# Routing of tokens to experts: small operands moved from SBUF to a PSUM bank

## The chip, the core and the metric

The kernel runs on one core of a Trainium2 chip. The core has five engines that work side by side, each on its own list of instructions in order: TensorE (PE, matrix products), VectorE (DVE), ScalarE (ACT), GpSimd (POOL) and SyncE (SP, which issues transfers). SBUF is the working memory of 128 partitions. PSUM is a smaller memory of 8 banks, 2 KB a partition each, into which TensorE writes and which VectorE and ScalarE read and write. The metric is device time in microseconds of one execution, the median of several.

## The reference

Attention with pooled queries, then a mixture of 8 experts with a fixed room of 576 tokens each:

```python
q_pool = q.reshape(B, H, S // 2, 2, D).mean(axis=3)        # B = H = 8, S = 1152, D = 64
scores = q_pool @ k.transpose(0, 1, 3, 2) / sqrt(D)
x = softmax(scores) @ v                                     # -> N = 4608 tokens of 512
logits = x @ w_gate                                         # [4608, 8]
for idx in argsort(-logits.flatten()):                      # best fit first
    tok, e = idx // E, idx % E
    if assigned[tok] >= 0 or counts[e] >= cap: continue     # cap = 576
    assigned[tok] = e; counts[e] += 1
for e in range(E):
    out[assigned == e] = relu(x[assigned == e] @ w1[e]) @ w2[e]
```

All is computed to nearly full fp32 accuracy: a product of two fp32 matrices is made as three products of their upper and lower parts.

## The kernel before

Two stages follow each other: attention (until about 1045 us) and the experts. The change lies in the second, in `experts`.

**Routing without a sort.** The greedy assignment is computed expert by expert, in the order in which experts fill up; `route(k)` finds the k-th expert to fill and its 576 tokens. Token scores lie as 128 partitions x 36 blocks (J = 36) x 8 experts in L. A penalty PEN per expert closes those that are full. `best` (L741 to L745) takes of each token the best open expert: LM = L + PEN, mx = its maximum, T1 = where LM equals mx, times e8 (a number for each expert), and r8 = the largest, which names the expert. `keys` (L747 to L755) turns the 36 scores of a partition into whole numbers with the same order (ki), in two halves of 16 bits, as floats in kf. Then eight search rounds, four on each half, narrow a threshold by one hexadecimal digit each. One round is a chain between VectorE and TensorE:

- VectorE: GE = keys against 16 thresholds (L789, 128x576 numbers); beside the next step it subtracts the threshold found so far from the keys (L820), and once, L824, joins the halves.
- TensorE: counts per expert and threshold, 5 small products into rb (L796).
- VectorE: keeps the own blocks (dg, L800) and adds them up (red, L802). TensorE: sums over partitions (L806).
- VectorE: which experts are full at which threshold (L810), a transpose (fars, L813), the digit found (got, L816, with half32, a table of 5 numbers), whose sum `base` starts the next round's L789.

After eight rounds `close` (L848 to L855) names the expert (re) and its tokens (gt, mine, asg), `members` and `prefix` (G, PS) number them, ST (L912, four operations of 128x640) and 20 small products into tb (L917) look up which token comes at which place, and L921 to L928 write the list idx. `shut`, `taken`, `left` and `settle` (PEN, CAPS, U, room L977) prepare the next expert.

**Products.** For each expert, GpSimd gathers weights and 576 tokens by idx (indirect DMA). ScalarE rounds them to upper parts (W1H, W2H, XH), GpSimd makes the lower parts of the weights by subtraction (W1L, W2L, L1095: 16 subtractions of 128x512 for each expert) and of half of the tokens from the third expert on (XL, L1045); VectorE makes the others. The tokens of the first two experts are turned by TensorE in five blocks (L1002) and subtracted by VectorE (L1011). TensorE then makes the products of the first layer (ph, L1112) and of the second (po, L1142 and L1139).

**Order.** `Order.emit` fixes the order in which each engine gets its instructions: a planner that gives each group a duration in ns and hands groups out as engines that wait for nothing else would begin them. So the routing of expert k+1 is interleaved with the products of expert k. The engines do not reorder: a count on TensorE that waits for GE holds all products behind it.

**PSUM before.** rb (counts and sums) and tb (the lookups, and the fifth token block when tokens are turned by TensorE) are a bank each; ph has four, po two. The eight banks are in use. All operands of the routing chain other than rb and tb lie in SBUF.

Of the kernel before, what the change touches and what calls it, by code (L numbers as in the profile page):

```python
# [26 lines left out]
M = S // 2              # pooled queries of a head  # L27
NKB = S // 128          # key blocks of a head
E, DM, F = 8, H * D, 1024
N = B * M               # tokens  # L30
CAP = N // E
NPAIR = B * H // 2      # pairs of heads: the same head of two batches
NSTEP = 2 * NKB         # key blocks of a pair
NB = 2 * M // 128       # token blocks of a pair of batches
NBLK = N // 128
SHIFT = 16.0 * 8.0 * math.log(2.0)   # weights are carried times 2^8


class Order:
    """Instructions in groups, with the memory that each reads and writes. `emit` hands them out in the  # L40
    order in which engines that wait for nothing else would begin them."""
# [92 lines left out]
# when parts of a pair's work come, in steps; which part goes first (steps) and how long a part's users give it (ns)  # L134
# [16 lines left out]
def routing_tables(nc, pool, ident, jp, scratch, do):  # L151
    """constants of the routing; `scratch`: whole numbers that are needed only here"""
# [31 lines left out]
    def order():  # L184
        V.tensor_scalar(C["before"], jp, 0.0, None, op0=OP.is_gt)                       # [k, m]: k < m
        V.tensor_scalar(C["upto"], jp, 0.0, None, op0=OP.is_ge)                         # [k, m]: k <= m
        V.tensor_copy(C["e8"], it8)                                                     # E - e
        V.tensor_copy(C["pcol"], it["p"])
        V.tensor_copy(C["pcol2"], it["p2"])
    do("DVE", 700, order)  # L190

    def digits():
        for t in range(4):                                          # (1 .. 16) * 16^t; the last never counts
            V.tensor_scalar(C["nib"][:, t], it["16"], float(16 ** t), None, op0=OP.mult)
            V.memset(C["nib"][:, t, 15:16], 3e9)
        V.tensor_scalar(C["nib"][:, 4], it["16"], -1.0, None, op0=OP.add)               # 0 .. 15
        k1 = scratch.bitcast(F32)[:, at:at + 64]
        V.tensor_scalar(k1, it["d"], 0.0, None, op0=OP.is_ge)                           # [16 j + t, 8 j + e]
        V.tensor_scalar(C["diag"], it["d"], 16.0, None, op0=OP.is_lt)
        V.tensor_tensor(C["diag"], C["diag"], k1, op=OP.mult)  # L200
        V.tensor_scalar(it["m"], it["m"], 15, None, op0=OP.bitwise_and)
        V.tensor_scalar(C["same16"], it["m"], 0.0, None, op0=OP.is_equal)               # [16 j + t, 16 r + t]
    do("DVE", 1500, digits)

    def places():
        V.tensor_copy(C["slots"], it["s"])
        V.tensor_copy(C["slot1"], it["s1"])                                             # 1 + slot
        V.tensor_scalar(C["jval"], it["s"][:, :J], 128.0, None, op0=OP.mult)            # 128 j
        for z in range(2):
            V.tensor_copy(C["TAB"][:, z, J + 1:J + 2], it["p"])                         # ranks, offset, partition  # L210
# [4 lines left out]
def attention(ctx, tc, top, kt, qt, v, wg, x_dram, L, npair=NPAIR):  # L215
# [7 lines left out]
    # ---- constants  # L223
# [48 lines left out]
    ndiag = const.tile([128, NB, 64], F32, name="ndiag")            # -1 at [64 + i, i, :]  # L272
# [23 lines left out]
    # ---- exact split of queries and keys into parts of 12 bits  # L296
# [45 lines left out]
    # ---- values in two parts, scaled by a power of two so that half precision's range holds them  # L342
    def values(n, t):
# [4 lines left out]
        # only the power of two counts  # L348
# [18 lines left out]
    # ---- maxima of the scores, [query, key] order  # L367
    NA = AT["na"]       # token blocks whose scores ScalarE moves out; VectorE reads the others in place

    def max_chunk(n, j, c, z, t):  # L370
        i = n % 2
        banks = [(ma, "ma"), (mb, "mb")]
        if n == 0:      # nothing else needs memory yet
# [28 lines left out]
    def aug(n, t):  # L402
# [3 lines left out]
        if n == 0:      # a row of each block of queries  # L406
# [6 lines left out]
        else:           # one row, brought there by DMA  # L413
# [8 lines left out]
    # ---- one key block: scores, weights, weighted values  # L422
    LAG = AT["lag"]

    def step(g):
# [27 lines left out]
        def weighted(js):  # L453
            for j in js:
                # bank 0: blocks 0..2; bank 1: the remainder, block 3
# [6 lines left out]
                for y, z in enumerate((1, 0) if j in (2, 4) else (0, 1)):  # L462
                    # second part times first parts only
# [35 lines left out]
    # ---- the gate's part of two heads, and their columns of x  # L499
# [12 lines left out]
    def gate(n, t):  # L512
        """three groups of columns of TensorE side by side; the sum stays turned until a batch is done"""
# [29 lines left out]
    def gate_last(n, q, t):  # L543
        """the last two heads: added at once"""
# [25 lines left out]
    # ---- the order of things  # L570
    od.cur = None
    for _ in range(AT["wu"]):        # TensorE's clock is up when the first products come
        od.add(-70, "PE", 60, lambda: nc.tensor.matmul(mb[:, :128], ones, ones, start=True, stop=True), w=["mb"])
    for _ in range(AT["wv"]):        # and is still up when the scores come
# [36 lines left out]
    for n in range(1, npair, 2):  # L611
        od.cur = None
        g = NSTEP * n + NSTEP
        if n + 1 < npair:
            # between the heads, when the weighted values' memory is free
# [24 lines left out]
# which work of an expert goes first (f.), how long users give it (ns), how it is divided  # L640
# [5 lines left out]
def experts(ctx, tc, x_dram, L, w1, w2, out, C):  # L646
# [13 lines left out]
    # ---- state of the assignment  # L660
    U = one([128, J], F32, "U")                     # not assigned yet
    asg = one([128, J], BF, "asg")                  # assigned to, as E minus its number
    mine = one([128, J], BF, "mine")
    CAPS = one([128, E], F32, "CAPS")               # room that is left
    PEN = one([128, E], F32, "PEN")                 # closed experts
# [3 lines left out]
    nc.vector.memset(PEN, 0.0)  # L669

# [4 lines left out]
    mx = one([128, J], F32, "mx")  # L675
    r8 = one([128, J], BF, "r8")
# [3 lines left out]
    kf = one([128, 2, J], F32, "kf")  # L680
# [6 lines left out]
    half32 = one([128, 5], F32, "half32")  # L687
# [3 lines left out]
    gt = one([128, 2, J], BF, "gt")  # L691
# [3 lines left out]
    G = one([128, 2, J], F32, "G")  # L695
# [18 lines left out]
    # first parts of 576 tokens, second parts of the last 64 and of the other 512  # L714
# [5 lines left out]
    rb = psum.tile([128, 512], F32, name="rb")  # L720
    tb = psum.tile([128, 512], F32, name="tb")
# [3 lines left out]
    TB = [("tb", c) for c in range(5)]  # L725

    def bj(ap, n=E):        # [128, J] over n
        return ap[:, :, None].to_broadcast([128, J, n])

    def be(ap):             # [128, E] over J  # L730
        return ap[:, None, :].to_broadcast([128, J, E])

    def first_of(mask8, out8, r1):
        """the first expert of a mask, one-hot; r1: E minus its number"""
        V.tensor_tensor(sm[:, 5], mask8, e8[:, 0], op=OP.mult)
# [3 lines left out]
    def best(dve, f):  # L739
        """of each token the best expert that is open, as E minus its number, and how well it fits"""  # L740
# [3 lines left out]
        dve(220, lambda: V.tensor_tensor(T1, T1, e8, op=OP.mult), ["T1"], ["T1"], f)  # L744
        dve(370, lambda: V.tensor_reduce(r8, T1, axis=AX.X, op=OP.max), ["T1"], ["best"], f)  # L745

    def keys(dve, f):  # L747
        """the order of floats as that of whole numbers, in two halves of 16 bits"""
# [3 lines left out]
        dve(106, lambda: V.tensor_tensor(ki[:, 0], ki[:, 0], b, op=OP.bitwise_xor), ["mx", "ki"], ["ki"], f)  # L752
        dve(90, lambda: V.tensor_scalar(ki[:, 1], ki[:, 0], 16, None, op0=OP.arith_shift_right), ["ki"], ["ki1"], f)
        dve(90, lambda: V.tensor_scalar(ki[:, 0], ki[:, 0], 0xFFFF, None, op0=OP.bitwise_and), ["ki1"], ["ki"], f)
# [464 lines left out]
```

## Time and profile before

| | |
|---|---|
| three runs | 1628.81, 1636.2, 1640.48 us, median 1636.2 |
| profiled execution, span | 1634.9 us |
| TensorE busy over the span | 1476.2 us (90%) |
| VectorE busy | 1254.1 us (77%) |
| GpSimd busy | 926.7 us (57%) |
| mean granted TensorE clock | 0.963 |
| expert stage, 1045 to 1635 us: TensorE busy | 506.15 of 590 us |

The trace covers one execution, from the first to the last instruction. A row of a group names line, engine, operation, output and inputs with shapes, the number of instructions, their busy time in us and the mean of one in ns, then the idle time of the engine ahead of them and what ended it. A timeline row gives start and duration in us; in brackets stands how long the engine had been idle and what released it. L numbers are lines of the kernel before.

### The profile page before, as it was taken

The page shows a single profiled execution, that of the slowest core. Times are in us where ns is not written, and L with a number is a line of the kernel's source. Part 1 is how long each engine was busy: PE and PEld are TensorE (multiplying, and loading weights), DVE is VectorE, ACT ScalarE, POOL GpSimd, SP SyncE. Part 2 cuts the span into 40 slices and gives each one's busy share as a digit, 9 for nine tenths or more (in the row PEclk, how much of TensorE's full clock was granted, in tenths as well). Part 3 has the DMA queues.
Part 4 walks back from the last instruction along what each step waited for, and adds up shares of the span by engine and source line. Part 5 has one row for each costly group of instructions (what it writes and reads, how often), then busy time and mean ns, then how long its engine had stood idle before and what let it go on. Part 6 is the DMA issues. An engine that isn't in the chain of part 4 may idle for free.

```text
span 1634.9 us, 32933 instructions
## 1 busy us (share of the span) xinstructions
PE 1476.2 (90%) x12535; PEld 1223.8 (75%) x12535; DVE 1254.1 (77%) x2636; ACT 898.5 (55%) x1801; POOL 926.7 (57%) x821
## 2 busy tenths in 40 slices
PE   7899999999999999999999999779588879899997
PEld 5677877877777777777778778567476767779995
DVE  7998898888888889978989986588887788753310
ACT  4776777777777777767677776222322222233431
POOL 4575566566566657656656666134644554557641
PEclk8999999999999999999999999899898989899999
DMA  9784676667676766856767752032132434333400
GB/s 235 188 184 117 159 175 156 148 155 172 158 162 157 177 141 155 197 126 165 189 135 164 169 112 48 15 132 90 73 139 86 134 127 134 114 116 119 147 30 30
DMA packets 123515, 221.97 MB, mean 136 GB/s; under 512 B 49500, under 2 KB 74076, under 8 KB 121180
## 3 DMA queue, kind: packets, MB, share of 16 engines
q1 hardware_dynamic: 114876, 167.40, 43.6%
q0 software_dynamic: 8336, 52.44, 9.0%
q8 instruction: 99, 1.62, 0.4%
q14 instruction: 60, 0.49, 0.1%
q10 hardware_dynamic: 144, 0.02, 0.0%
HBM read 99.63 MB, written 18.87 MB: 72 GB/s over the span
## 4 chain that ended last, share of the span: by engine, by line
PE 50%; DVE 37%; DMA 6%; issue 4%; ACT 1%; POOL 1%; SPq 0%; another core or an unknown queue 0%; POOLq 0%; DVEq 0%; ACTq 0%
PE av L464 12%; PE ph L1112 11%; PE po L1142 9%; DVE MS L392 6%; DVE PM L448 5%; PE sc L436 4%; DVE MX L380 4%; PE sc L439 4%; PE ma L376 3%; DVE KL L323 3%; PE mb L376 3%; DVE got L816 2%; DVE RS L486 2%; DMA VD<-in_v_dram 2%; DVE QL L303 2%
## 5 line engine op out<-in xcount | busy, mean ns | idle before, releaser
L448 POOL TENSOR_TENSOR PM<-P 128x576 f16<-128x576 f32 x383 | 523.5, 1377 | 295.8 <-ACT P L444 292.1
L464 PE MATMUL av<-V,P 128*128 128x129 f16 (+1 forms) x2880 | 442.8, 225 | 0.7 <-DVE V L363 0.5
L444 ACT ACTIVATE P<-sc 128x576 f32<-128x576 f32 x576 | 370.5, 657 | 93.4 <-PE sc L439 84.0
L464 PE MATMUL av<-V,PM 128*128 128x65 f16 (+1 forms) x2880 | 364.7, 198 | 0.0
L464 PEld LDWEIGHTS <-P 128*128 128x128 bf16 (+1 forms) x2880 | 258.2, 100 | 75.6 <-issue 12.8
L464 PEld LDWEIGHTS <-PM 128*128 128x128 f16 (+1 forms) x2880 | 259.9, 100 | 48.1 <-issue 0.5
L436 PE MATMUL sc<-QA,KA 128*128 128x288 f32 x1152 | 265.0, 312 | 0.1
L439 PE MATMUL sc<-QB,KB 65*128 65x288 f32 (+1 forms) x1152 | 251.0, 300 | 3.9 <-issue 3.9
L392 DVE TENSOR_TENSOR MS<-MS 128x1728 bf16<-128x1728 bf16 (+3 forms) x256 | 232.2, 907 | 12.5 <-ACT MS L384 8.8
L448 DVE TENSOR_TENSOR PM<-P 128x576 f16<-128x576 f32 x193 | 196.7, 1019 | 40.5 <-ACT P L444 40.5
L384 ACT CAST MS<-mb 128x384 bf16<-128x384 f32 x314 | 151.3, 482 | 96.7 <-PE mb L376 94.8
L436 PEld LDWEIGHTS sc<-QA,KA 128*128 128x128 f32 x1152 | 196.6, 193 | 4.8 <-ACT P L444 0.4
L376 PE MATMUL mb<-KH,BD 128*128 128x384 f32 x407 | 158.6, 390 | 38.7 <-DVE MX L380 26.2
L439 PEld LDWEIGHTS sc<-QB,KB 65*128 65x128 f32 (+1 forms) x1152 | 189.6, 193 | 4.1 <-issue 4.1
L376 PE MATMUL ma<-KH,BD 128*128 128x384 f32 x438 | 172.5, 394 | 20.6 <-DVE MX L380 20.3
L1142 PE MATMUL po<-W2H,HX 128*128 128x512 f32 x512 | 166.7, 402 | 0.5 <-ACT OT L1147 0.5
L384 ACT CAST MS<-ma 128x384 bf16<-128x384 f32 x250 | 120.2, 481 | 78.8 <-PE ma L376 75.2
L1112 PE MATMUL ph<-XL,W1H 128*128 128x320 f32 (+1 forms) x512 | 159.8, 312 | 2.1 <-DVE XL L1011 2.1
L1112 PE MATMUL ph<-XH,W1H 128*128 128x320 f32 (+1 forms) x512 | 160.6, 314 | 0.6 <-DVE XL L1011 0.6
L1112 PE MATMUL ph<-XH,W1L 128*128 128x320 f32 (+1 forms) x512 | 160.4, 313 | 0.0
L1117 ACT ACTIVATE HX<-ph 128x256 fp32r<-128x256 f32 (+1 forms) x128 | 52.4, 410 | 192.5 <-PE ph L1112 176.6
L1142 PE MATMUL po<-W2L,HX 128*128 128x512 f32 (+1 forms) x320 | 130.3, 407 | 0.0
(233 smaller groups left out, 2561.7 us busy)
## 6 DMA issues: line engine op xcount, KB each, us to landing
QD<-in_qt_dram SPq DMA_DIRECT2D x32, 576.0 KB
KD<-in_kt_dram SPq DMA_DIRECT2D x64, 288.0 KB
VD<-in_v_dram SPq DMA_DIRECT2D x32, 576.0 KB
KA<-KH SPq DMA_DIRECT2D x64, 288.0 KB
KB<-KH SPq DMA_DIRECT2D x64, 288.0 KB
QA<-QH SPq DMA_DIRECT2D x128, 144.0 KB
KA<-KL SPq DMA_DIRECT2D x64, 288.0 KB
QB<-QL SPq DMA_DIRECT2D x64, 144.0 KB
```

The lines of the kernel that those rows point to most:

```text
L376: od.add(t, "PE", 162, lambda: nc.tensor.matmul(m[:, :384], BD[i][:, j, :], KH[i][:, 384 * c:384 * c + 384], start=True, stop=True), r=[(" ...
L380: od.add(t, "DVE", 465, lambda: nc.vector.tensor_reduce(MX[i][:, j, c:c + 1], m[:, :384], axis=AX.X, op=OP.max), r=[mk], w=[("MX", i, j, c ...
L384: od.add(t, "ACT", 371, lambda: nc.scalar.copy(MS[b][:, j % 3, 384 * c:384 * c + 384], m[:, :384]), r=[mk], w=[("MS", b, j % 3, c)], tag="mc")
L392: od.add(t + .01 * z, "DVE", 72 + .52 * w * rows, lambda w=w: nc.vector.tensor_tensor(m[:, :, :w], m[:, :, :w], m[:, :, w:2 * w], op=OP.ma ...
L436: nc.tensor.matmul(c[:, t, :288], KA[i][:, s, ks], QA[i][:, s, 288 * t:288 * t + 288], start=True, stop=False)
L439: nc.tensor.matmul(c[:, t, :288], KB[i][:kr, s, ks], QB[i][:kr, s, 288 * t:288 * t + 288], start=False, stop=True)
L444: od.add(g + 0.1, "ACT", 531, lambda: nc.scalar.activation(p.rearrange("p (a b) -> p a b", a=2), c[:, :, :288], AF.Exp, scale=1.0 / 16), r ...
L448: od.add(g + 0.2, en, dur, lambda: eng.tensor_tensor(pm, p, hi, op=OP.subtract), r=[("P32", g % NP)], w=[("PM", g % NM)], tag="pm" + "DP"[ ...
L464: nc.tensor.matmul(o[:, D * z:], (hi, pm)[z][:, q0:q0 + w], rhs[:, D * z:], start=first and kb == 0 and y == 0, stop=kb == NKB - 1 and y = ...
L1112: nc.tensor.matmul(p, a[:, d, fs], b[:, d, qs], start=z == 0, stop=z == 11)
L1117: nc.scalar.activation(HH[:, f, qs], p, AF.Relu)
L1142: nc.tensor.matmul(o[:n], a[:, z, q0:q0 + n], b[:, z], start=z == 0 and y == 0, stop=z == 7, skip_group_check=True)
```

## The change

A PSUM bank, `kb`, is set aside for VectorE alone, and pieces of it hold the routing chain's small operands: mine, PEN, mx, r8, kf, half32, gt and G move there from SBUF, and four new pieces are added: e8p and pcolp (copies of a row of e8 and of pcol), sm1 (a second copy of the mask of the expert just closed) and kx (the keys as whole numbers, ahead of their split in two). Each two-input operation of the chain then has at most one input in SBUF. T1 is multiplied by e8p, an fp32 row repeated over the blocks, in place of the bf16 table e8. Of the keys only the upper half is copied to kf; `lower` reads the lower half from ki. ST, room and the token subtractions keep their SBUF operands.

To free the bank, rb and tb become parts of one bank, rt: columns 0 to 127 and 128 to 511. The fifth token block is turned in a bank of the products instead (ph[0][1] for the first expert, ph[0][0] for the second). The planned durations of some of these groups are changed. The rest of the difference is comments that are left out.

```diff
+    kb = psum.tile([128, 512], F32, name="kb")
+    used = [0]
+    def bank(*shape):
+        n = math.prod(shape)
+        x = kb[:, used[0]:used[0] + n]
+        used[0] += n
+        return x.rearrange("p (a b) -> p a b", b=shape[1]) if len(shape) > 1 else x
-    mine = one([128, J], BF, "mine")
+    mine = bank(J)
-    PEN = one([128, E], F32, "PEN")
+    PEN = bank(E)
+    e8p = bank(E)
+    sm1 = bank(E)
+    nc.vector.tensor_copy(e8p, e8[:, 0])
-    mx = one([128, J], F32, "mx")
-    r8 = one([128, J], BF, "r8")
+    mx = bank(J)
+    r8 = bank(J)
-    kf = one([128, 2, J], F32, "kf")
+    kx = bank(J).bitcast(I32)
+    kf = bank(2, J)
-    half32 = one([128, 5], F32, "half32")
+    half32 = bank(5)
-    gt = one([128, 2, J], BF, "gt")
+    gt = bank(2, J)
-    G = one([128, 2, J], F32, "G")
+    G = bank(2, J)
-    rb = psum.tile([128, 512], F32, name="rb")
-    tb = psum.tile([128, 512], F32, name="tb")
+    rt = psum.tile([128, 512], F32, name="rt")
+    rb, tb = rt[:, :128], rt[:, 128:]
+    pcolp = bank(1)
+    V.tensor_copy(pcolp, pcol)
...
-        dve(220, lambda: V.tensor_tensor(T1, T1, e8, op=OP.mult), ["T1"], ["T1"], f)
+        dve(370, lambda: V.tensor_tensor(T1, T1, be(e8p), op=OP.mult), ["T1"], ["T1"], f)
...
-        dve(106, lambda: V.tensor_tensor(ki[:, 0], ki[:, 0], b, op=OP.bitwise_xor), ["mx", "ki"], ["ki"], f)
-        dve(90, lambda: V.tensor_scalar(ki[:, 1], ki[:, 0], 16, None, op0=OP.arith_shift_right), ["ki"], ["ki1"], f)
-        dve(90, lambda: V.tensor_scalar(ki[:, 0], ki[:, 0], 0xFFFF, None, op0=OP.bitwise_and), ["ki1"], ["ki"], f)
-        dve(110, lambda: (V.tensor_copy(kf, ki), V.memset(base, -32768.0)), ["ki", "ki1"], ["key", "base"], f)
+        dve(150, lambda: V.tensor_tensor(kx, ki[:, 0], b, op=OP.bitwise_xor), ["mx", "ki"], ["kx"], f)
+        dve(150, lambda: V.tensor_scalar(ki[:, 1], kx, 16, None, op0=OP.arith_shift_right), ["kx"], ["ki1"], f)
+        dve(150, lambda: V.tensor_scalar(ki[:, 0], kx, 0xFFFF, None, op0=OP.bitwise_and), ["kx"], ["ki"], f)
+        dve(200, lambda: (V.tensor_copy(kf[:, 1], ki[:, 1]), V.memset(base, -32768.0)), ["ki", "ki1"], ["key", "base"], f)
...
-                V.tensor_tensor(W, e8, bj(ru), op=OP.is_equal)
+                V.tensor_tensor(W, be(e8p), bj(ru), op=OP.is_equal)
...
-                        V.scalar_tensor_tensor(kf[:, 0], kf[:, 1], 65536.0, kf[:, 0], op0=OP.mult, op1=OP.add)
+                        V.scalar_tensor_tensor(kf[:, 0], kf[:, 1], 65536.0, ki[:, 0], op0=OP.mult, op1=OP.add)
...
-            V.tensor_tensor(widx[k], re[:, 1:2], pcol, op=OP.add)
+            V.tensor_tensor(widx[k], re[:, 1:2], pcolp, op=OP.add)
...
+                V.tensor_scalar(sm1, e8[:, 0], re[:, 0:1], None, op0=OP.is_equal)
-            dve(340, shut, ["re"] + ([("ST", LT["cs"], 3)] if not k else []), ["PEN", "sm"], LT["fb"])
+            dve(500, shut, ["re"] + ([("ST", LT["cs"], 3)] if not k else []), ["PEN", "sm"], LT["fb"])
-                V.scalar_tensor_tensor(CAPS, sm[:, 1], 1e9, CAPS, op0=OP.mult, op1=OP.add)
+                V.scalar_tensor_tensor(CAPS, sm1, 1e9, CAPS, op0=OP.mult, op1=OP.add)
...
-                     (ph[1][1], [("ph", 1, 1)]), (tb, TB)][c] if not k else (
-                         (ph[c // 2][c % 2], [("ph", c // 2, c % 2)]) if c < 4 else (tb, TB))
+                     (ph[1][1], [("ph", 1, 1)]), (ph[0][1], [("ph", 0, 1)])][c] if not k else (
+                         ph[c // 2 % 2][c % 2], [("ph", c // 2 % 2, c % 2)])
```

Two places of the order show what moves. The first is VectorE at the end of the fourth expert's routing, where the lookup tables ST are made. The kernel before (po and ph numbers name the bank):

```order
L902 COPY of<-rb 128x4
L903 CAST TAB<-rb 128x2
L741 TENSOR_TENSOR LM<-L,PEN 128x288
L912 TENSOR_SCALAR ST<-slots,of 128x640 x4
L970 TENSOR_TENSOR CAPS<-CAPS,rb 128x8
L971 SCALAR_TENSOR_TENSOR CAPS<-sm,CAPS 128x8
L975 SCALAR_TENSOR_TENSOR U<-gt,U 128x36
L977 TENSOR_SCALAR room<-PS,of 128x36
```

The kernel after, whose lines are some 17 higher and where kb stands for every operand in the new bank:

```order
L919 COPY of<-rt 128x4
L920 CAST TAB<-rt 128x2
L758 TENSOR_TENSOR LM<-L,kb 128x288
L929 TENSOR_SCALAR ST<-slots,of 128x640 x4
L1169 TENSOR_TENSOR OT_13596<-po_13602,O_13593 64x512
L1139 SCALAR_TENSOR_TENSOR HX<-ph_13598,HX 128x256
L988 TENSOR_TENSOR CAPS<-CAPS,rt 128x8
L989 SCALAR_TENSOR_TENSOR CAPS<-kb,CAPS 128x8
L938 TENSOR_TENSOR ixf<-slot_164,rt 128x5
```

ST stays where it was, ahead of the same small operations; two operations of the products (OT, HX) now come between, and room comes behind the index operations (L938 to L945). The second place is TensorE at the second expert's fifth token block. Before, it was turned in tb amid the first products:

```order
L796 MATMUL rb<-W,GE 64x32
L1002 MATMUL tb<-ident,XG 128x64 x4
L1112 MATMUL ph_13605<-XH,W1L 128x256
L1112 MATMUL ph_13605<-XH,W1H 128x256
L1112 MATMUL ph_13605<-XL,W1H 128x256
L1112 MATMUL ph_13605<-XH,W1L 128x256
L1112 MATMUL ph_13607<-XH,W1H 128x256
```

After, it is turned in ph_13598, the bank in which the first block was turned:

```order
L1130 MATMUL ph_13600<-XH,W1H 128x256
L1130 MATMUL ph_13600<-XL,W1H 128x256
L1130 MATMUL ph_13600<-XH,W1L 128x256
L1020 MATMUL ph_13598<-ident,XG 128x64 x4
L813 LDWEIGHTS GE
L813 MATMUL rt<-W,GE 128x64
```

The first twelve products go to another bank, ph_13600, ahead of it, and the count follows it instead of standing ahead. Around the search rounds the order keeps its pattern: a count, seven or eight products, the sum over partitions, some sixteen products, the next count (half as many in the second layer).

More of the change, by code (lines that the diff above doesn't have):

```diff
@@ L733, in first_of @@
     def first_of(mask8, out8, r1):
-        V.tensor_tensor(sm[:, 5], mask8, e8[:, 0], op=OP.mult)
+        V.tensor_tensor(sm[:, 5], mask8, e8p, op=OP.mult)
         V.tensor_reduce(r1, sm[:, 5], axis=AX.X, op=OP.max)
```

## The prediction

> **What bounds the kernel now.** I read the page's parts 1 and 2 first, then the expert stage in windows, then who TensorE waits for there, and last the durations of the instructions it waits for. The attention stage ends near 1045 us and the change does not touch it. The windows below (engine busy, then granted clock, DMA share, GB/s) split what follows: 1096 to 1460 us is the stretch in which six experts' routing runs beside the products of the experts before them, 1115.6 to 1126.5 a piece of it without any GpSimd work, and 1470 to 1623 the products of the last three experts, when all routing is done.
>
> ```profile
> core 0: us, PE busy (x) PEld busy (x) DVE busy (x) ACT busy (x) POOL busy (x), PEclk, DMA share, GB/s
> 1096.00:1460.00 364.00, 306.87 (x1940) 257.22 (x1939) 292.45 (x943) 99.14 (x209) 181.54 (x182) 0.92 0.32 108
> 1115.60:1126.50 10.90, 10.90 (x89) 10.23 (x88) 8.66 (x36) 2.46 (x6) 0.00 (x0) 1.00 0.01 2
> 1470.00:1623.00 153.00, 153.00 (x911) 138.27 (x910) 33.94 (x84) 51.82 (x111) 81.55 (x87) 1.00 0.26 88
> ```
>
> Without routing TensorE never pauses and its clock is 1.00. With routing it stands idle 364.00 - 306.87 = 57.1 us, and its mean clock is 0.92. But in the 10.90 us of routing without GpSimd it does not pause either: routing as such costs no idle time. What TensorE waits for between 1096 and 1460 us (total, times, longest):
>
> ```profile
> PE rb L796 <- DVE GE L789: 33.8, 15, 10.2
> PE rb L806 <- DVE red L802: 8.3, 6, 4.2
> PE tb L917 <- DVE ST L912: 4.7, 3, 3.5
> PE rb L796 <- DVE W L782: 4.1, 1, 4.1
> PE rb L878 <- DVE tot L873: 3.2, 1, 3.2
> PE rb L878 <- DVE re L891: 1.9, 1, 1.9
> PE po L1142 <- ACT OT L1147: 0.5, 1, 0.5
> ```
>
> Nearly all of it is VectorE's routing chain. TensorE takes its work in order, so a count (L796) whose masks GE are late holds up the expert products queued behind it. Why the chain is late stands in the durations of its instructions (ns, min/median/max):
>
> ```profile
> L816 DVE SCALAR_TENSOR_TENSOR got<-fars,half x49: 191/193/11398, 1052.0 to 1429.8; 128x32 f32<-128x32 f32 x49
> L820 DVE TENSOR_SCALAR kf<-kf,base x56: 229/243/4986, 1050.0 to 1431.4; 128x36 f32<-128x36 f32 x56
> L789 DVE SCALAR_TENSOR_TENSOR GE<-kf,base,nib x56: 771/819/1767, 1049.2 to 1430.0; 128x576 bf16<-128x576 f32 x56
> L912 DVE TENSOR_SCALAR ST<-slots,of x48: 244/375/5697, 1074.9 to 1451.1; 128x640 f16<-128x640 f16 x28, 128x128 f16<-128x128 f16 x20
> ```
>
> An instruction on 32 numbers takes 0.19 us or 11.4 us. The timeline at the longest shows what else runs:
>
> ```profile
> 1170.17 11.40 DVE L816 SCALAR_TENSOR_TENSOR got<-fars,half 128x32 f32<-128x32 f32 x1
> 1170.46 1.30 POOL L1095 TENSOR_TENSOR W1L<-W,W1H 128x512 fp32r<-128x512 f32 x1
> 1171.72 9.80 POOL L1095 TENSOR_TENSOR W2L<-W,W2H 128x512 fp32r<-128x512 f32 x8
> 1182.49 0.56 PE L796 MATMUL rb<-W,GE 128*128 128x64 bf16 x5 [10.15 <-DVE GE L789]
> ```
>
> It ends (1181.57) as the ninth GpSimd subtraction in a row ends (1181.52): VectorE waits out GpSimd's whole run, and TensorE then waits 10.15 us. The Trainium skill, page "SBUF — State Buffer", section "Who interferes with whom", gives a rule for this: a VectorE instruction with two SBUF inputs, or in a two-port mode, shuts out a GpSimd instruction that reads SBUF and is shut out by it, and one with at most one SBUF input does not contend. By that rule, the trace agrees as to who is hit, but the wait was nine instructions long, 11.4 us, not one of 1.3.
>
> **The change, term by term.** The sum is made on the profiled span, 1634.9 us, 1.3 under the runs' median of 1636.2; savings are taken off the median.
>
> Ceiling: 57.1 us idle, and the clock. A mean of 0.92 over 364 us is 29.1 us of lost rate; spread as the busy time is (306.87/364), it cost work 24.5 us. Together 81.6.
>
> Not touched: the waits for ST (4.7), for re (1.9) and for ScalarE (0.5), 0.6 that the list does not name, and 3.0 of the GE row, where VectorE waits for a ScalarE that has no instruction:
>
> ```profile
> 1277.09 0.71 ACT L1117 ACTIVATE HX<-ph 128x256 fp32r<-128x256 f32 x2 [3.93 <-remote]
> 1277.50 0.42 DVE L1121 SCALAR_TENSOR_TENSOR HX<-ph,HX 128x256 fp32r<-128x256 f32 x1 [2.86 <-ACT HX L1117]
> ```
>
> That is 10.7 us, with a clock share of 24.5/57.1 = 0.43 per us 15.3. Left: 66.3. These are waits behind L816 (half32 goes to PSUM), L820, L824, L851 (kf), L789 (kf), L753, L754 (kx) and L743, L781, L782 (mx, r8, e8p), and in the changed kernel none of them reads two SBUF operands or copies SBUF to SBUF.
>
> Ahead of the window, the second routing starts beside the first token blocks' subtractions:
>
> ```profile
> 1087.96 2.75 DVE L743 TENSOR_TENSOR T<-LM,mx 128x288 bf16<-128x288 f32 x1
> 1090.64 0.68 DVE L1011 TENSOR_TENSOR XL<-ph,XH 128x512 fp32r<-128x512 f32 x1
> ...
> L741 DVE TENSOR_TENSOR LM<-L,PEN 128x288 f32<-128x288 f32 x7 | 3.2, 458 | 0.0
> ```
>
> The first products need XL, queued behind T. T's undisturbed time is that of LM, of the same form (458 ns), so XL comes 2.3 us sooner; I take 2.0.
>
> What VectorE pays for PSUM:
>
> ```profile
> L744 DVE TENSOR_TENSOR T<-T,e 128x288 bf16<-128x288 bf16 x7 | 2.1, 304 | 0.0
> L1011 DVE TENSOR_TENSOR XL<-ph,XH 128x512 fp32r<-128x512 f32 x6 | 4.1, 681 | 0.0
> L1095 DVE TENSOR_TENSOR W1L<-W,W1H 128x512 fp32r<-128x512 f32 x2 | 1.4, 688 | 1.6 <-ACT W1H L1092 1.6
> ...
> L891 DVE TENSOR_SCALAR re<-re x8: 145/148/153, 1074.5 to 1449.1; 128x1 f32<-128x1 f32 x8
> ```
>
> - Reads: a subtraction with one operand in PSUM takes 681 ns, with both in SBUF 688. I take no difference.
> - The product with e loses its 16-bit form: 304 goes to about LM's 458 ns, +0.15 us an expert; in the first expert, where nothing runs beside routing, it is on the path. The Trainium skill, page "VectorE: DVE Perf Modes", section "Why PSUM operands drop a tier", says the same: an operand in PSUM limits fp32 to one element a cycle; by it this costs what the row says.
> - Writes to PSUM by VectorE: no row shows one. From below, an SBUF write's time; from above, a small operation's fixed time paid twice, +0.15 us (re, one number, L891). Some 15 stand in the first expert's path: 0 to 2.2 us; nearest are the 36-number rows, so 0.5. In later experts rounds hide them: kf's subtraction (L820) lies beside the count on TensorE.
> - The second mask, sm1 (+0.1), and one fifth token block turned in a bank of the products (ph instead of tb): there the order puts twelve products between the bank's first use and its second, so about 0.6 of waiting. First expert and this together: 1.4 us. Fewer keys are copied (36 instead of 72), worth nothing here: the copy lies ahead of W's wait.
>
> What still waits, afresh: ST keeps slots in SBUF, room (L977) is an SBUF-to-SBUF scalar operation, and XL of later experts (L1045) subtracts two SBUF operands.
>
> ```profile
> L912 DVE TENSOR_SCALAR ST<-slots,of 128x640 f16<-128x640 f16 x28 | 16.8, 661 | 0.0
> L977 DVE TENSOR_SCALAR room<-PS,of x7: 235/239/1273, 1085.3 to 1443.5; 128x36 f32<-128x36 f32 x7
> L1045 DVE TENSOR_TENSOR XL<-XG,XH 128x512 fp32r<-128x512 f32 x12 | 10.6, 901 | 6.2 <-ACT XH L1041 6.1
> ```
>
> ST waits 28 x (661 - 375) = 8.0 us over seven experts, 1.1 a group, of which 4.7 (0.59) reaches TensorE. Today a blocked key operation ahead often leaves room and XL a free port; now they meet GpSimd themselves. Six groups of room at 1.1: 6.9, less the 1.0 of its largest wait, x 0.59 = 3.5 us, with clock 5.0. The same GpSimd work in a sixth less time raises ST's own share by 1.0. XL: 12 x 0.21 = 2.5 us of waiting may double, 1.5 reaching TensorE.
>
> Rounds without a block still end with TensorE and VectorE close together: one had a gap of 0.21, the row at 1115.6 none.
>
> ```profile
> 1106.32 0.42 PE L796 MATMUL rb<-W,GE 128*128 128x64 bf16 x5 [0.21 <-DVE GE L789]
> ```
>
> Half of that for each of the 21 rounds whose wait goes (15 and 6 in the list): 2.2.
>
> Sum: 66.3 + 2.0 - 1.4 - 5.0 - 1.0 - 1.5 - 2.2 = 57.2. 1636.2 - 57.2 = 1579.0 us. Then TensorE bounds the stage, as it does from 1470 on, and GpSimd can feed it: there it keeps up at 153/3 = 51 us an expert and is busy 81.55 of the 153 us.
>
> **Rivals.**
> - The wait moves to what is left in SBUF. For it: one ST took 5697 ns, and each of the keys' long waits shows what a group that comes in the midst of a run pays. If each of the 13 groups of ST and room waits 4 us, that is 52 us of VectorE, x 0.59 = 31 of TensorE, x 1.43 = 44 with the clock; 4.7 x 1.43 + 5.0 + 1.0 = 12.7 of it are counted above, so 31 more: 1610 us. Against it: the seven groups of ST average 1.1 today.
> - All of it goes, ST's waits falling into TensorE's slack: 1636.2 - 81.6 = 1555, up to 1562.
> - The shared bank. rb and tb now lie in one bank, rt. The Trainium skill, page "PSUM — Partial Sum Buffer", section "PSUM bank collisions raise a hardware error", says that two engines must be kept apart by bank and not by address; by it every count must wait for the index operations' reads of tb and these for the counts. As a mechanism here: up to 1.5 us of reading (L921 to L928) each way, twice for seven experts, 21 us: about 1601. Against it: no such wait stands in today's list, and in the order the next count comes some 20 products or more behind the lookups.
> - Not the operands. If VectorE waited for GpSimd's use of something else, nothing changes: 1636. Against it: VectorE's instructions of one tensor input in the same rounds, beside the same GpSimd runs, never wait:
>
> ```profile
> L813 DVE STREAM_TRANSPOSE fars<-far x49: 163/211/214, 1051.7 to 1429.6; 128x32 f32<-128x32 f32 x49
> L802 DVE TENSOR_REDUCE red<-dg x56: 257/264/274, 1050.9 to 1432.1; 128x8 f16<-128x64 f16 x56
> ```
>
> - Slower: PSUM access by VectorE is dear. Some 2 operations in each of 56 rounds and 15 in each of 7 experts are serial, 217; from 57.2/217 = 0.26 us each the gain is gone, at 0.35 it is 76 us: 1655. Against it: 681 beside 688 ns.
>
> **How the numbers follow.** Forecast 0.66 (its own range 1564 to 1596, by the PSUM writes and by what ST, room and XL do), wait moved 0.12, all gone 0.08, bank 0.05, nothing 0.05, dear PSUM 0.04. From 1560 to 1612 leaves out the last two and most of "all gone", some 0.15. About 1% is what a measurement of this kernel can tell from no change (under 1619.8 is faster): faster 0.66 + 0.12 + 0.08 + 0.05 = 0.91, same 0.05, slower 0.04.
>
> **What the changed profile would show.** Right: the operation that replaces L816 has a maximum under 0.4 us, also beside GpSimd's runs; waits of counts for GE fall from 33.8 to under 8 us; the clock in the routing stretch rises to 0.97 or more; the ST maximum stays at some us and is the largest wait left. Wrong: medians of GE or got more than 0.1 us longer (dear PSUM), counts that wait for index reads (bank), or 0.19 us operations still at several us (not the operands). If ST and room wait over 25 us together, the wait has moved.

## The result, and the profile after

| | before | after |
|---|---|---|
| median | 1636.47 us | 1577.37 us |
| four runs each | 1628.81 to 1640.48 | 1568.15 to 1580.79 |
| profiled execution, span | 1634.9 us | 1566.3 us |
| mean granted clock | 0.963 | 0.978 |
| VectorE busy over the span | 1254.1 us | 1196.1 us |

The ratio is 0.9635, interval 0.9596 to 0.9674: 59.1 us less between the medians.

The profiled execution of the changed kernel is the fastest of its four (1568.15 us), and the spans differ by more than the medians, by 68.6 us. Of that, 6.8 us lie in the attention stage, which the change does not touch: the first expert's first operation begins at 1045.8 us before and at 1039.0 after. So the expert stage alone is compared, from this operation to the end of the last product. First the kernel before, one window (length, then busy time of TensorE, its weight loads, VectorE, ScalarE and GpSimd, granted clock, DMA share, GB/s):

```profile
1045.80:1623.60 577.80, 506.14 (x3164) 428.93 (x3164) 369.06 (x1201) 162.02 (x341) 281.48 (x286) 0.94 0.31 104
```

The kernel after, the whole stage and the routing stretch in it:

```profile
1039.00:1555.00 516.00, 487.43 (x3164) 415.21 (x3164) 310.16 (x1206) 161.86 (x341) 276.92 (x286) 0.97 0.35 116
1096.00:1400.00 304.00, 289.35 (x1913) 243.14 (x1912) 231.02 (x921) 99.24 (x209) 177.58 (x184) 0.97 0.40 134
```

The stage takes 61.8 us less. TensorE does the same 3164 instructions; it is busy 506.14 - 487.43 = 18.7 us less, because its clock rose from 0.94 to 0.97 (busy time times clock is about the same, 476 and 473 us), and idle 71.66 - 28.57 = 43.1 us less. In the routing stretch 14.65 us of idle time are left where 57.1 stood. What TensorE waits for there (1090 to 1400 us; total, times, longest):

```profile
PE rt L895 <- DVE tot L890: 6.4, 3, 3.4
PE rt L813 <- DVE GE L806: 3.5, 2, 2.2
PE ph L1130 <- DVE XL L1063: 2.1, 1, 2.1
PE rt L985 <- DVE idx L945: 1.3, 2, 0.8
PE rt L985 <- DVE TAB L920: 1.1, 1, 1.1
PE ph L1130 <- DVE HX L1142: 0.2, 1, 0.2
```

The counts' wait for GE fell from 33.8 us to 3.5; the waits for red, ST, W and re are gone. tot, which had 3.2 us before, now leads: it is the cast of the last column of the prefix sums, two numbers a partition, ahead of a small product. The durations (ns, min/median/max) of the operations that the prediction spoke of, and of tot:

```profile
L833 DVE SCALAR_TENSOR_TENSOR got<-fars,kb x49: 149/189/190, 1045.8 to 1368.7; 128x32 f32<-128x32 f32 x49
L837 DVE TENSOR_SCALAR kb<-kb,base x56: 222/260/267, 1043.8 to 1370.7; 128x36 f32<-128x36 f32 x56
L806 DVE SCALAR_TENSOR_TENSOR GE<-kb,base,nib x56: 774/818/820, 1043.0 to 1369.5; 128x576 bf16<-128x576 f32 x56
L890 DVE CAST tot<-PS x8: 171/175/3874, 1068.4 to 1387.3; 128x2 bf16<-128x2 f32 x8
L929 DVE TENSOR_SCALAR ST<-slots,of x48: 243/376/502, 1069.1 to 1388.9; 128x640 f16<-128x640 f16 x28, 128x128 f16<-128x128 f16 x20
L995 DVE TENSOR_SCALAR room<-PS,of x7: 232/234/3441, 1079.8 to 1383.1; 128x36 f32<-128x36 f32 x7
```

got's longest was 11398 ns and is 190: not one of the 49 waits any more, nor does any GE or any subtraction from the keys. The operations that keep their operands in SBUF do not all behave alike: ST, whose longest was 5697, is at 502; room's longest rose from 1273 to 3441, and tot reaches 3874. The timeline shows tot's longest beside a GpSimd run of three subtractions (start, duration; in brackets the idle time ahead and what ended it):

```profile
1273.42 3.87 DVE L890 CAST tot<-PS 128x2 bf16<-128x2 f32 x1
1273.56 3.70 POOL L1113 TENSOR_TENSOR W2L<-W,W2H 128x512 fp32r<-128x512 f32 x3
...
1277.35 0.17 PE L895 MATMUL rt<-tot,before 128*128 128x2 bf16 x1 [3.44 <-DVE tot L890]
```

The cast ends when the third subtraction does, and TensorE stands 3.44 us. room, twelve microseconds later, shows its price at another place:

```profile
1282.91 6.29 POOL L1113 TENSOR_TENSOR W2L<-W,W2H 128x512 fp32r<-128x512 f32 x5
...
1285.80 3.44 DVE L995 TENSOR_SCALAR room<-PS,of 128x36 f32<-128x36 f32 x1
...
1294.48 0.42 PE L813 MATMUL rt<-W,GE 128*128 128x64 bf16 x5 [2.17 <-DVE GE L806]
```

Nobody waits for room itself. But the next expert's chain stands behind it on VectorE, and its first GE comes late: 2.17 of GE's 3.5 us are room's. (In the experiment below that frees room, only GE's other wait, 1.4 us, is left.)

The two waits for idx are new as well. The longer one:

```profile
1170.79 0.67 DVE L983 TENSOR_REDUCE ng<-WG 128x8 bf16<-128x288 bf16 x1
1172.77 0.17 PE L985 MATMUL rt<-ng,mones 128*128 128x8 bf16 x1 [0.84 <-DVE idx L945]
```

The product L985 needs ng, which is done at 1171.46, but it waits until idx (1172.71) has read its lookups. idx is no input of this product; the two share only the bank rt, one writing and the other reading it. In the kernel before, with two banks, this product waits for no index operation in any of its seven turns. By this, sharing the bank costs 1.3 us of idle time in this stretch; it was not tried by itself.

### The profile page after: what moved, and what is told of

Same layout as the page of the kernel before. It is cut to its first block, busy times and chain, and to the rows that moved or that the text cites. A ratio compares the mean times of both kernels' runs of the same rounds, so it can differ in the third digit from the quotient of the medians.

```text
span 1566.3 us, 32939 instructions
## 1 busy us (share of the span) xinstructions
PE 1452.2 (93%) x12535; PEld 1206.5 (77%) x12535; DVE 1196.1 (76%) x2645; ACT 897.4 (57%) x1801; POOL 925.4 (59%) x821
## 4 chain that ended last, share of the span: by engine, by line
PE 57%; DVE 33%; DMA 5%; issue 3%; ACT 1%; POOL 1%; SPq 0%; POOLq 0%; DVEq 0%; ACTq 0%
PE av L464 13%; PE ph L1130 13%; PE po L1160 11%; DVE MS L392 7%; DVE PM L448 5%; PE sc L436 5%; DVE MX L380 4%; PE sc L439 4%; PE ma L376 4%; DVE KL L323 3%; PE mb L376 3%; DVE RS L486 2%; DVE QL L303 2%; DVE V L363 2%; DVE QS L299 1%
## 5 line engine op out<-in xcount | busy, mean ns | idle before, releaser
L464 PEld LDWEIGHTS <-P 128*128 128x128 bf16 (+1 forms) x2880 | 257.8, 100 | 75.4 <-issue 12.1
L1130 PE MATMUL ph<-XL,W1H 128*128 128x320 f32 (+1 forms) x512 | 156.6, 306 | 2.8 <-DVE XL L1063 2.1
L1130 PE MATMUL ph<-XH,W1H 128*128 128x320 f32 (+1 forms) x512 | 156.4, 305 | 0.4 <-ACT XH L1027 0.2
L1130 PE MATMUL ph<-XH,W1L 128*128 128x320 f32 (+1 forms) x512 | 156.5, 306 | 0.0
L1135 ACT ACTIVATE HX<-ph 128x320 fp32r<-128x320 f32 (+1 forms) x128 | 52.5, 410 | 153.9 <-PE ph L1130 151.7
```

What stands on the lines that cost most here:

```text
L464: nc.tensor.matmul(o[:, D * z:], (hi, pm)[z][:, q0:q0 + w], rhs[:, D * z:], start=first and kb == 0 and y == 0, stop=kb == NKB - 1 and y = ...
L1130: nc.tensor.matmul(p, a[:, d, fs], b[:, d, qs], start=z == 0, stop=z == 11)
L1135: nc.scalar.activation(HH[:, f, qs], p, AF.Relu)
```

## The experiments

All are made from the changed kernel. Their line numbers are those of the kernel after, up to five higher where lines were added. For most, the window row of the expert stage is shown, with the columns as above. Ratios are to the kernel before, run beside them.

**The changed kernel again.** To know how much of a difference of a few microseconds is chance, the same kernel ran once more beside the others.

> The changed kernel once more, beside the next two on the same chip: 1570 to 1585 us by every theory.

Six runs: median 1577.78 us, ratio 0.9648 (0.9615 to 0.968). Its profiled span is 1574.0 us, 7.7 longer than that of the first profile, but its expert stage takes 515.60 us, 0.4 less. The difference lies ahead of the experts. Between these two profiles a stage's length is much firmer than a span, and the experiments below are read by it.

**All operands back in SBUF.**

```diff
-    kb = psum.tile([128, 512], F32, name="kb")
+    kb = one([128, 512], F32, "kb")
```

The order of the instructions is the same on every engine; only the place of the operands differs.

> The changed kernel with one line different: kb, the place of the small operands, is an SBUF tile again. Order of every engine, operations, types and the shared bank rt are those of the changed kernel. Theory (what counts is that VectorE reads two operands from SBUF, or copies SBUF to SBUF, beside GpSimd's subtractions): the time of the kernel before comes back, 1625 to 1645 us, and the digit operation (got) has a maximum of several us again. Rival (the gain came with the new order and planned durations, or with the bank shared by rb and tb): it stays under 1590 us.

Ten runs: median 1634.66 us, ratio 0.9973 (0.9944 to 1.0002). Its stage, by the window and the groups (number of instructions, then busy us and mean ns of one):

```profile
1048.30:1621.30 573.00, 505.54 (x3164) 427.96 (x3164) 362.50 (x1207) 161.73 (x341) 281.63 (x286) 0.93 0.31 105
...
L806 DVE SCALAR_TENSOR_TENSOR GE<-kb,base,nib 128x576 bf16<-128x576 f32 x56 | 63.4, 1133 | 1.5
L833 DVE SCALAR_TENSOR_TENSOR got<-fars,kb 128x32 f32<-128x32 f32 x49 | 30.0, 613 | 1.5
...
L890 DVE CAST tot<-PS x8: 170/172/4248, 1076.8 to 1453.6; 128x2 bf16<-128x2 f32 x8
L929 DVE TENSOR_SCALAR ST<-slots,of x48: 240/375/562, 1077.5 to 1455.2; 128x640 f16<-128x640 f16 x28, 128x128 f16<-128x128 f16 x20
```

The time before is back. So it is the place of the operands that makes the gain. The shared bank rt, the moved fifth block, the second mask and the other order are all still in this kernel, and together they are worth between nothing and 9 us by the interval, 4.8 us by the two stages. The last two rows (ns, min/median/max) show something that the operands' place does not explain: already here tot has a long wait, and ST has none. In the kernel before, tot never waited:

```profile
L873 DVE CAST tot<-PS x8: 171/172/176, 1074.2 to 1449.0; 128x2 bf16<-128x2 f32 x8
```

So the wait went from ST to tot with the new order (or another of the parts that this kernel keeps), not with the move to PSUM. With room it is the other way round: here its longest is 304 ns, so its 3441 ns came with the move itself, as the prediction had argued.

**The operand of got alone in PSUM.** got had the longest waits before. If one operation's wait could be taken away by itself, moving half32 would bring a good part of the gain.

```diff
-    kb = psum.tile([128, 512], F32, name="kb")
+    kb = one([128, 512], F32, "kb")
+    kp = psum.tile([128, 512], F32, name="kp")
-    half32 = bank(5)
+    half32 = kp[:, :5]
```

> kb in SBUF, only half32 (second input of got) in PSUM. In the kernel before, got's waits were 49 x (859 - 193) ns = 32.6 us of some 71 us of VectorE's waits in the routing chain. If waits add up by operation: 46% of the gain of 59 us, about 27 us, 1609 us. If a wait that got no longer pays is paid by the next operation that reads two from SBUF (GE, 0.2 us later, then kf's subtraction): less than 10 us gained, over 1626 us, and the means of GE and of kf's subtraction rise.

Four runs: median 1625.77 us, ratio 0.9899 (0.9852 to 0.9946).

```profile
1050.80:1615.90 565.10, 500.61 (x3164) 424.41 (x3164) 358.11 (x1207) 161.48 (x342) 284.83 (x286) 0.94 0.32 106
...
L807 DVE SCALAR_TENSOR_TENSOR GE<-kb,base,nib 128x576 bf16<-128x576 f32 x56 | 75.5, 1349 | 1.5
L834 DVE SCALAR_TENSOR_TENSOR got<-fars,kp 128x32 f32<-128x32 f32 x49 | 9.1, 185 | 1.5
...
1164.94 13.38 DVE L807 SCALAR_TENSOR_TENSOR GE<-kb,base,nib 128x576 bf16<-128x576 f32 x1
1165.47 2.48 POOL L1114 TENSOR_TENSOR W1L<-W,W1H 128x512 fp32r<-128x512 f32 x2
1167.91 9.79 POOL L1114 TENSOR_TENSOR W2L<-W,W2H 128x512 fp32r<-128x512 f32 x8
```

Against the kernel with everything in SBUF, got is rid of 30.0 - 9.1 = 20.9 us of waiting. GE, the next operation with two operands in SBUF, takes on 75.5 - 63.4 = 12.1 of them; 8.8 are left, and the stage is 573.0 - 565.1 = 7.9 us shorter. The handing on can be seen at a run of four subtractions, first with everything in SBUF, then with half32 in PSUM:

```profile
1156.45 5.01 POOL L1113 TENSOR_TENSOR W1L<-W,W1H 128x512 fp32r<-128x512 f32 x4
1157.86 3.66 DVE L833 SCALAR_TENSOR_TENSOR got<-fars,kb 128x32 f32<-128x32 f32 x1
...
1155.45 5.01 POOL L1114 TENSOR_TENSOR W1L<-W,W1H 128x512 fp32r<-128x512 f32 x4
1156.92 0.19 DVE L834 SCALAR_TENSOR_TENSOR got<-fars,kp 128x32 f32<-128x32 f32 x1
1157.15 3.93 DVE L807 SCALAR_TENSOR_TENSOR GE<-kb,base,nib 128x576 bf16<-128x576 f32 x1
```

got passes, and GE, right behind it, waits in its place. GE's longest wait, 13.38 us at a run of ten in the first block, is not new: with everything in SBUF it met such a run too, and its longest was 12392 ns. The median fell below the 1626 us from which the second theory counted, by 0.2 us only; between the two the profile decides, and there more than half of the wait is handed on.

**The keys alone in PSUM.**

```diff
-    kb = psum.tile([128, 512], F32, name="kb")
+    kb = one([128, 512], F32, "kb")
+    kp = psum.tile([128, 512], F32, name="kp")
-    kf = bank(2, J)
+    kf = kp[:, :2 * J].rearrange("p (a b) -> p a b", b=J)
```

> kb in SBUF, only kf (input of GE, kf's subtraction, the joining of halves and the last comparisons) in PSUM. If waits add up by operation: kf's share before was 12.7 + 4.4 + 7.2 + 4.7 = 29 of 71 us, 41% of the gain, 24 us, 1612 us. If they are passed on: under 10 us gained, over 1626 us, and got's mean rises above 859 ns.

Four runs: median 1607.65 us, ratio 0.9828 (0.9778 to 0.9877). The stage takes 548.5 us, 24.5 less than with everything in SBUF. Here GE is at its undisturbed time, and got waits more than it did:

```profile
L807 DVE SCALAR_TENSOR_TENSOR GE<-kp,base,nib 128x576 bf16<-128x576 f32 x56 | 45.6, 815 | 1.5
L834 DVE SCALAR_TENSOR_TENSOR got<-fars,kb 128x32 f32<-128x32 f32 x49 | 38.8, 792 | 1.5
```

The gain is of the size that adding up gave (24 us). But got took on 38.8 - 30.0 = 8.8 us, which adding up does not have, and its mean stayed under the 859 ns that the other theory asked for, though it rose from the 613 of the kernel with everything in SBUF. So neither theory holds as it was put.

**All but got's operand in PSUM.** The counterpart: of the search round, only got is left in SBUF.

```diff
-    half32 = bank(5)
+    half32 = one([128, 5], F32, "half32")
```

> The changed kernel with half32 alone back in SBUF, so got is the one operation of a search round that reads two from SBUF. If waits add up by operation: 27 us lost, about 1604 us. If one such operation in a round of 3.5 us is enough to meet nearly every run of GpSimd's subtractions: 40 to 55 us lost, 1617 to 1632 us. If got is only late where others are late too: under 1590 us.

Four runs: median 1607.78 us, ratio 0.9799 (0.976 to 0.9838).

```profile
1054.70:1600.90 546.20, 495.95 (x3164) 420.83 (x3164) 336.89 (x1205) 161.68 (x341) 276.55 (x286) 0.95 0.33 110
...
L833 DVE SCALAR_TENSOR_TENSOR got<-fars,half 128x32 f32<-128x32 f32 x49 | 38.7, 791 | 1.5
```

One operand of five numbers, left behind in SBUF, costs 546.2 - 515.6 = 30.6 us, half of the gain. got waits 38.7 - 9.1 = 29.6 us, about as much as the stage loses. That is near the 27 us of adding up, and far from the 40 to 55 of an operation that meets nearly every run.

The four together: moving half32 alone brings 7.9 us, moving all else without it 573.0 - 546.2 = 26.8, and both 573.0 - 515.6 = 57.4. The two parts add up to 34.7; the other 22.7 come only when both are moved. Both theories, that the parts add up and that the wait is only passed on, were too simple. One susceptible operation in a round, left alone, still brings about half of the waiting: in its stage VectorE is busy 336.89 us, 26.7 more than in the changed kernel (310.16), where everything in SBUF makes it 52.3 more (362.50). A second one in the same round adds less than it would alone.

**The operands that the change left.** tot and room get a second input in PSUM in place of an SBUF-to-SBUF copy or scalar operation; room's product goes to PSUM, so that the subtraction from U has one input there; the first of the two masks reads e8p.

```diff
-    room = one([128, J], F32, "room")
+    room, room2, capj, zero2 = one([128, J], F32, "room"), bank(J), bank(J), bank(2)
+    nc.vector.memset(capj, float(CAP))
+    nc.vector.memset(zero2, 0.0)
-            V.tensor_copy(tot, PS[:, :, J - 1])
+            V.tensor_tensor(tot, PS[:, :, J - 1], zero2, op=OP.add)
-                V.tensor_scalar(sm[:, 1], e8[:, 0], re[:, 0:1], None, op0=OP.is_equal)
+                V.tensor_scalar(sm[:, 1], e8p, re[:, 0:1], None, op0=OP.is_equal)
-                V.tensor_scalar(room, PS[:, 1], of[:, 1:2], float(CAP), op0=OP.add, op1=OP.is_le)
-                V.tensor_tensor(room, room, G[:, 1], op=OP.mult)
-                V.tensor_tensor(U, U, room, op=OP.subtract)
+                V.scalar_tensor_tensor(room, PS[:, 1], of[:, 1:2], capj, op0=OP.add, op1=OP.is_le)
+                V.tensor_tensor(room2, room, G[:, 1], op=OP.mult)
+                V.tensor_tensor(U, U, room2, op=OP.subtract)
```

> The changed kernel, and the operations on which its waits are left also read at most one operand from SBUF and none is a copy within SBUF: tot is the prefix sums plus a zero in PSUM, room compares with a row in PSUM, its product goes to PSUM, the closed expert's mask reads e8p. Only ST and the token subtractions (XL) still can wait. If the waits of tot (6.4 us of TensorE) and room (3.4 us at most) go for good: with the clock 8 to 12 us less than the changed kernel, 1565 to 1569 us. If they pass on to ST and XL, which come right after them: within 4 us of the changed kernel.

Six runs: median 1569.43 us (1566.42 to 1573.55), ratio 0.9595 (0.9562 to 0.9627). The changed kernel beside it had 1577.78 (1574.83 to 1581.1), so this one is 8.3 us faster, and its stage is 12.0 us shorter than in the changed kernel's second profile. It beats both kernels. The window, three groups, and the longest waits of TensorE in the routing stretch (1104 to 1413 us):

```profile
1053.00:1556.60 503.60, 483.94 (x3164) 412.37 (x3164) 301.04 (x1205) 161.93 (x341) 277.95 (x286) 0.98 0.35 119
...
L931 DVE TENSOR_SCALAR ST<-slots,of 128x640 f16<-128x640 f16 x28 | 11.2, 460 | 0.0
L997 DVE SCALAR_TENSOR_TENSOR room<-PS,of,kb 128x36 f32<-128x36 f32 x7 | 1.7, 242 | 0.0
L892 DVE TENSOR_TENSOR tot<-PS,kb 128x2 bf16<-128x2 f32 x8 | 1.3, 157 | 0.3
...
PE ph L1132 <- DVE XL L1065: 2.1, 1, 2.1
PE rt L987 <- DVE idx L947: 1.9, 2, 1.1
PE rt L815 <- DVE GE L808: 1.4, 1, 1.4
```

tot and room run at their own length now. TensorE no longer waits for tot here, and the next GE is no longer late for room: in all 5.7 us of waiting are left in this stretch where 14.6 stood. ST, which keeps all its operands in SBUF, averages 460 ns where the changed kernel's first profile has 390: 28 x 70 = 2.0 us were handed on to it, little of what tot and room had waited.

**GpSimd writes only.** All so far moves VectorE's operands. This moves GpSimd's: everything of VectorE's is back in SBUF, and GpSimd makes the lower parts of the weights by writing zeros, at the same places of the order, so that it reads nothing there. The products of these lower parts are thereby left out of the outputs.

```diff
-    kb = psum.tile([128, 512], F32, name="kb")
+    kb = one([128, 512], F32, "kb")
-                    od.add(tt, en, dur, lambda o=lo[p], a=raw[p], b=hi.bitcast(F32)[p], eng=eng: eng.tensor_tensor(
-                        o, a, b, op=OP.subtract), r=[key, (nm + "H", z, y)], w=[(nm + "L", z, y)], first=first, late=LT["lw"])
+                    def low(o=lo[p], a=raw[p], b=hi.bitcast(F32)[p], eng=eng):
+                        if eng is V:
+                            eng.tensor_tensor(o, a, b, op=OP.subtract)
+                        else:
+                            for _ in range(2):
+                                eng.memset(o.bitcast(F32), 0.0)
+                    od.add(tt, en, dur, low, r=[key, (nm + "H", z, y)], w=[(nm + "L", z, y)], first=first, late=LT["lw"])
```

> kb in SBUF, and GpSimd's subtractions for the weights are each replaced by two memsets of the same output, which read nothing (the lower weight parts are zero, so outputs lack their products). If GpSimd's reading is what shuts VectorE's second SBUF input out: got and GE stay at their minimum (maximum of got under 0.4 us away from the remaining token subtractions), and the time falls to 1575 to 1590 us although all operands lie in SBUF; operations that copy SBUF to SBUF (kf's subtraction, ST) may still wait for writes. If any use of SBUF by GpSimd blocks: got keeps waits of a memset's length and more, and the time stays above 1600 us.

Four runs: median 1563.2 us, ratio 0.9552 (0.9511 to 0.9593), faster than either theory had it. Two memsets are shorter than the subtraction they replace (about 1.05 us by the rows below, against 1.2 to 1.3), so the time itself is no clean measure; the timeline is. First got and GE inside a run of memsets, then got beside a remaining subtraction of tokens (XL), then two operations from SBUF to SBUF with one tensor input, beside memsets:

```profile
1241.40 4.73 POOL L1118 MEMSET W1L<- 128x512 f32 x9
1244.42 0.15 DVE L833 SCALAR_TENSOR_TENSOR got<-fars,kb 128x32 f32<-128x32 f32 x1
1245.08 0.81 DVE L806 SCALAR_TENSOR_TENSOR GE<-kb,base,nib 128x576 bf16<-128x576 f32 x1
...
1258.54 1.41 DVE L833 SCALAR_TENSOR_TENSOR got<-fars,kb 128x32 f32<-128x32 f32 x1
1258.57 1.32 POOL L1063 TENSOR_TENSOR XL<-XG,XH 128x512 fp32r<-128x512 f32 x1
...
1159.35 2.17 POOL L1118 MEMSET W1L<- 128x512 f32 x4
1159.99 0.98 DVE L837 TENSOR_SCALAR kb<-kb,base 128x36 f32<-128x36 f32 x1
...
1223.90 4.54 POOL L1118 MEMSET W2L<- 128x512 f32 x8
1225.03 0.52 DVE L890 CAST tot<-PS 128x2 bf16<-128x2 f32 x1
```

The same got, with both inputs in SBUF, takes 0.15 us amid writes and 1.41 beside reads. It is so throughout the stage: the three gots and the three GEs that took over 0.1 us more than their medians (193 and 819 ns) all stand beside a subtraction of tokens, none beside memsets. So GpSimd's reading is what stops them. But the subtraction from the keys (0.98 us, elsewhere in this kernel 0.24) and tot (0.52, elsewhere 0.17) wait for writes too. This is the rule of the Trainium skill, page "SBUF — State Buffer", section "Who interferes with whom": VectorE shares a read and a write interface with GpSimd, its second SBUF input comes through the first, and copies and scalar operations in a two-port mode need the pair. The rows agree with it as to who waits for whom in each of these cases; in which mode an operation ran, no row shows.

## Why the prediction came out right, and which term did not

- **The cause.** It was taken to be the operands' place, and the order, the bank and the planned durations to be of little worth. Taking only the place back gave 0.9973 of the time before, so the rest is worth at most 9 us of the 59 by the interval. The rival in which VectorE waits for something else than its operands' place is out, and so is the dear access to PSUM: GE's median is 818 ns after, 819 before.
- **The sum.** Forecast 57.2 us, measured 59.1 between the medians and 61.8 in the stage. Taken apart, its terms were 46.4 + 2.0 - 1.4 - 3.5 - 1.0 - 1.5 - 2.2 = 38.8 us of idle time, and 18.4 of clock; the stage gave 43.1 and 18.7. That a waiting TensorE costs its clock too held nearly to the size.
- **Adding up.** The sum treated the waits behind each operand as one pool that goes as a whole. This was needed: had only the longest, got's, been moved, 7.9 us would have come of it.
- **The shared bank.** This rival came true in small: not the search counts but the product L985 waits for index reads, twice, 1.3 us, where the rival had 21 us of such waiting.
- **Ahead of the routing stretch.** T beside the first token blocks went from 2.75 us to 0.45. From the first operation of the stage to the third turned block's subtraction it takes 43.39 us after (1039.0 to 1082.39) where it took 44.84: 1.45 us gained. The prediction had +2.0, less most of 1.4 for the first expert. The product with e8p takes 451 ns for 304, as forecast from LM's row (458).
- **Writes to PSUM.** Taken at 0.5 us for the first expert. The subtraction from the keys went from a median of 243 ns to 260, 17 ns each; 15 such writes are 0.26 us.
- **The wrong step: who would still wait.** The prediction said that ST stays the longest wait, that 4.7 us for it are not touched, and that its share rises. After the change TensorE never waits for ST in the routing stretch; tot takes 6.4 us of its time. The list of what is left in SBUF had ST, room and XL, but not tot, which copies within SBUF too: its longest before was 176 ns, and an operation that had not waited was not asked whether it could. The prediction's own list of waits did have 3.2 us for tot, and the sum put them among those that go. That was right as to their cause, an operation ahead (gt, L851, which took 4.99 us from 1255.02 on), but with it tot left the account. The step's fault was to take it that GpSimd's runs would meet the same operation as before. They meet whatever stands there when they begin: with all operands still in SBUF but the new order, tot has 4248 ns and ST 562. The term for ST and room together was of about the right size (4.7 + 3.5 of idle and ST's 1.0, against tot's 6.4 and room's 2.2), but lay on another instruction; that the sum still fits is luck in this term. Giving tot and room operands in PSUM confirmed it: 12.0 us of the stage.
- **Also too cautious.** Of the 10.7 us of idle time called untouched, nothing can be found in the waits after under the old names but 0.2 for HX; idx (the shared bank, 1.3) and TAB (1.1) are new. The gain in idle time, a little above the forecast, fits this. Which part of the new order moved GpSimd's runs from ST to tot was not tried by itself and stays open.
- **XL.** Forecast to wait twice as long; its group's mean went from 901 to 1133 ns (900 with all operands back in SBUF), 12 x 452 = 5.4 us over the undisturbed 681 where 12 x 220 = 2.6 had been, and 2.1 of it reached TensorE, as against 1.5 forecast.

## What to carry to other kernels

Where an instruction's longest time is many times its median, look at what the other engine was doing in that stretch, and then list every operation of the chain by the place of its inputs and output, the tiny ones too: the longest waiter only hides those behind it. Taken away one by one, such waits bring less than together: got's operand alone brought 7.9 us and the keys alone 24.5, where all brought 57.4, and the one left behind cost 30.6. An operation of that kind which has not waited so far is not safe: a new order is enough for a run to meet it, as it met a cast that had never taken over 176 ns.

## What the chip showed that was not expected

- VectorE does not get in between GpSimd's subtractions that follow one another: GE began at 1164.94 us, and ended at 1178.32, 0.6 us after the last of ten (1177.70); its own work is 0.8 us. In the three cases shown (11.40, 13.38 and 3.87 us) VectorE's record even begins 0.29, 0.53 and 0.14 us before that of the first subtraction, and VectorE waits all the same; what held it at that moment is not shown. Beside memsets it does get in: tot, amid eight of them, was over after 0.52 us, about the length of one.
- A small size does not protect from the wait: a cast of two numbers a partition waited 3.87 us where the search round's 576 numbers, one input in PSUM, waited for nothing.
